# Rebuilding the prologue of a fused adaLN, attention and SwiGLU kernel: scale rows first, four head groups over half the keys, filler products

## The chip, the cores and the metric

The kernel runs on one core of a Trainium2 chip. The metric is the device time of one execution in microseconds (us). Three runs of the kernel before gave 1167.83, 1168.52 and 1172.24 us; the median, 1168.52 us, is the time before. The engines are named as the profile names them: PE (TensorE's matmuls), PEld (its weight loads), DVE (VectorE), ACT (ScalarE), POOL (GpSimd), SP (SyncE, which here issues nearly all DMAs).

## What is computed

```python
def reference(A_x, A_wq, A_wk, A_wv, A_wo, B_x, B_w1, B_w3, B_w2, c, w_mod):
    mod = (silu(c) @ w_mod).reshape(1, 6, 1, 1024)
    sa, ca, ga, sb, cb, gb = mod[:, 0], ..., mod[:, 5]      # shift, scale, gate; twice
    h = layernorm(x) * (1 + ca) + sa                        # x: 2048 tokens x 1024
    q = h @ wq   # 32 heads of 32      k = h @ wk, v = h @ wv   # one key and value head for all
    o = softmax(q k^T / sqrt(32)) v
    x = x + ga * (o @ wo)
    h = layernorm(x) * (1 + cb) + sb
    x = x + gb * ((silu(h @ w1) * (h @ w3)) @ w2)           # 1024 -> 3584 -> 1024
```

All tensors are bf16. The scale `1 + ca` and the shift `sa` are folded into the projections: the weights wq, wk and wv are multiplied by the scale, and the shift becomes a bias, `sa @ w`.

## The kernel before, in words

**A planner writes the order.** `build` adds every operation to a graph (`G.add`) with an engine, an estimated duration, a priority (`prio`, smaller is earlier) and the buffers it reads and writes. `Dag.schedule` (L106 to L260) plays the graph through with these estimates and fixes one order for each engine; `emit` writes the five instruction streams with semaphores. At run time each engine goes through its own list in order, and an instruction that has to wait holds up all that stand behind it. `LOOK` (L205) is a switch that lets the planner hold back a long DVE instruction; it is 0 in this version.

**Prologue (L452 to L762).** SP loads the 16 tiles of x (128 tokens each) into 8 slots of X and, between them, eight 128-row pieces of the first 2048 columns of w_mod, which hold the shift and the scale together (`ORDER`, L644). silu(c) is laid out by a small transpose (L495). DVE takes mean and variance (L509, L511; for tiles 3 and 6 ACT does it, L519 and L523), POOL the reciprocal root (L530, L532), DVE normalizes (L544), PE transposes (L558), and ACT or DVE copies the transposed tile to HT (L569, L572). The products with w_mod (L677) fill one bank; from it come `1 + ca` (L687) and the shift (L689). Then the bias products (L693, L699, L707, later L741), the scaling of wk, wv and wq (L719, L721, L750), the key projections (L608), the value projections (L619) and the query projections (L629). The gates and the second modulation follow (L782, L809, L787, L794).

**Attention (L830 to L959).** Eight blocks of 256 queries. For each block, eight head groups f of four heads. One *step* s takes 256 keys: eight score products (L855) into PSUM banks of SP, then two exponentials of 128x1024 on ACT (L865) into a ring U of 11 buffers. Eight steps make a head group. DVE adds the eight exponentials up in two trees (L879, L884) and folds these (L889); PE multiplies the exponentials by V (L902) and the tree sum by a 0/1 matrix SEL (L922), which gives the denominators. DVE copies both (L929, L937, L940), takes reciprocals (L946), spreads them (L952) and divides (L957). A block has 128 exponentials, the kernel 1024.

**Post (L982 to L1084).** For each block the product with wo (L996), the residual (L1000), the second layernorm, the gate and up products (L1030, 448 a block), tanh on ACT (L1039, 14 a block), the down products (L1064, 224 a block) and the output. Its weights stream through a ring of six buffers in WREG, HREG and X. The planner sets the post of block b among the attention steps of block b+1. Six PSUM banks belong to the scores once attention runs; everything else then shares banks 0 and 1.

Of the kernel before, what the change touches and what calls it, by code (L numbers as in the profile page):

```python
# [8 lines left out]
P = 128  # L9
# [3 lines left out]
LOOK = 0.0  # L13
# [15 lines left out]
class Dag:  # L29


    def __init__(self, nc):
        self.nc = nc
        self.nodes = []
        self.last_write = {}
        self.readers = {}
        self.seq = 0
        self.dma_sems = {}
        self.last_acq = {}
        self.chain = 0  # L40

# [64 lines left out]
    def schedule(self, banks):  # L106
# [41 lines left out]
        while left:  # L148
# [56 lines left out]
            if e == "dve" and LOOK and n.dur > 0.9 and n.prio > 1:  # L205
                fin = None
                for b in banks:
                    g = bank_group[b]
                    rem = [x for x in g.nodes if x.start is None and x.eng == "pe"] if g is not None else []
                    if rem:  # L210
                        f1 = t_free["pe"] + sum(x.dur for x in rem) + 0.26
                        if fin is None or f1 < fin:
                            fin = f1
                if fin is not None and t < fin < t + LOOK:
                    t_free["dve"] = fin
                    continue
            ready[e].remove(n)
# [132 lines left out]
def build(nc, x_in, wq_in, wk_in, wv_in, wo_in, w1_in, w3_in, w2_in, c_in, wmod_in, out, S, D, F):  # L350
# [34 lines left out]
    BP = (0, 0, 0)  # L385
    WP = (4, 4, 4)
    RP = (0, 0, 0)
# [6 lines left out]
    RB = sb("RB", [P, QB], F32)  # L394
    WKR = sb("WKR", [P, NC, 4, 32], BF16)
    ASB = XN[:, 2:4, :].rearrange("p a d -> p (a d)").bitcast(F32).rearrange("p (a q) -> p a q", a=4)
    DSB = WKR[:].rearrange("p c a f -> p (c a f)").bitcast(F32).rearrange("p (a q) -> p a q", a=2)
# [25 lines left out]
    NR = len(RING)  # L423
    assert NF * QB + 2 * 4096 <= NC * S and NXS == 8
# [5 lines left out]
    WQ0R = WKR[:].rearrange("p c a f -> p c (a f)")  # L430
    WQ0K = ["WKR"]
# [20 lines left out]

    cuts = {}
    G.add("pool", lambda e: e.memset(SEL[:], 0.0), writes=["SEL"], dur=0.3)
    for a, fs in enumerate(DGRP):
        edge = [32 * j // len(fs) for j in range(len(fs) + 1)]
        for j, f in enumerate(fs):
# [4 lines left out]
    G.add("pool", lambda e: e.memset(IDENT[:], 0.0), writes=["IDENT"], dur=0.2)  # L462
    G.add("pool", lambda e: e.affine_select(IDENT[:], IDENT[:], pattern=[[-1, P]], compare_op=ALU.not_equal,
                                            fill=1.0, base=0, channel_multiplier=1),
          reads=["IDENT"], writes=["IDENT"], dur=0.4)

# [5 lines left out]
    def xload(t0, n):  # L472
        r = []
        for t in range(t0, t0 + n):
            r.append(dma(lambda e, t=t: e.dma_start(X[:, t % NXS, :], x2[t * P:(t + 1) * P, :]),
                         ("x", t % NXS), writes=[("X", t % NXS)], nbytes=P * D * 2))
        return r

    WQK = [("WREG", "q")]
    xload(0, 8)  # L480

    def wmload(k, after=()):
        return dma(lambda e, k=k: e.dma_start(WM01[:, k, :], wmod_in[k * P:(k + 1) * P, 0:2 * D]), ("wm01", k),
            writes=[("UR", k)], nbytes=P * 2 * D * 2, after=after)
# [50 lines left out]
    def xnt(q):  # L535

        return XN[:, q, :] if q < 4 else UREG[:, (NU + NTR - 2) * 2048 + (q - 4) * D:][:, 0:D]

    def xnk(q):
        return [] if q < 4 else [("UR", NU + NTR - 2 + (q - 4) // 2)]  # L540

    def ln_norm(t, q, s=None, bp=0):
        s = t % NXS if s is None else s
        G.add("dve", lambda e: e.tensor_scalar(xnt(q), X[:, s, :], MV[:, t, 0:1], RS[:, t:t + 1],  # L544
                                               ALU.subtract, ALU.mult),
              reads=[("X", s), ("RS", t), ("MV", t)], writes=[("XN", q)] + xnk(q), dur=0.42, prio=2 - bp)

    def ln_transpose(nt, q0, dst, dkeys, fs, fm, engs, prio=5, cbs=None, allow=None, bp=0):
# [3 lines left out]
        for cb in range(NC // ncb) if cbs is None else cbs:  # L552
            g = grp(allow)
            for i in range(nt):
# [6 lines left out]
                G.add("pe", tr, reads=[("XN", q0 + i), "IDENT"] + xnk(q0 + i), dur=ncb * 0.065, lat=0.2,  # L561
# [41 lines left out]
    def kproj(t0, n, allow=None):  # L603
        sl = slice(t0, t0 + n)

        def kmm(e, b, c):
            for gg in range(4):
                r = e.matmul(b[32 * gg:32 * gg + 32, 0:n], WKV[:, 0, c, :], HT[:, c, sl], start=c == 0, stop=c == NC - 1,  # L608
                             tile_position=(0, 32 * gg), skip_group_check=True)
            return r  # L610
        g = mm_group(NC, kmm, lambda c: WKK + hk(c, t0, n), n_cols=n, allow=allow, mode="V")
        G.add("dve", lambda e, g=g: e.tensor_scalar(KT[:, sl], PB[g.bank][:, 0:n], BIA[:, 0:1], None, ALU.add),
              reads=[("BIA", 0)], writes=[("KT", t) for t in range(t0 // 256, (t0 + n) // 256)], groups=[(g, "r")],
              dur=dve_t(n), prio=-5)

    def vproj(tb):
        def vmm(e, b, i):
            tt, c = i // NC, i % NC
            return e.matmul(b[:, tt * 32:(tt + 1) * 32], HT[:, c, tb * 512 + tt * P:tb * 512 + (tt + 1) * P],  # L619
                            WKV[:, 1, c, :], start=c == 0, stop=c == NC - 1)  # L620
        g = mm_group(4 * NC, vmm, lambda i: WVK + hk(i % NC, tb * 512, 512), n_cols=64, per=NC)
# [5 lines left out]
    def qproj(t0, n, f, allow=None):  # L627
# [3 lines left out]
                     lambda c: [("WQ", min(f, 1), c)] + hk(c, t0, n) + WQK, n_cols=n, allow=allow)  # L631
        G.add("dve", lambda e, g=g: e.tensor_scalar(QT[:, f, sl], PB[g.bank][:, 0:n], BIA[:, f + 1:f + 2], None, ALU.add),
              reads=[("BIA", min(f + 1, 2))],
# [5 lines left out]
    ONACT = (3, 6)  # L639
    TR2A, TR2B = (0, 1, 2, 3), ()  # L640
    Q1ST = 1
    TR2E = ("act",)
    TR3E = ("act",)
    ORDER = ("w0", "w1", "w2", "w3", "x8", "x9", "w4", "x10", "x11", "w5", "w6", "w7", "q", "x12", "x13", "x14", "x15")  # L644

    def ln(t):
        (ln_stats_act if t in ONACT else ln_stats)(t)
        ln_scale(t, 1)
        ln_norm(t, t % 8)

    def tr(t0, nt, cbs, engs, allow=None):
        G.chain = 3
        ln_transpose(nt, t0 % 8, lambda c: HT[:, c, t0 * P:(t0 + nt) * P], lambda c: htk(c, t0 * P, nt * P), None, None,
                     engs, cbs=cbs, allow=allow)
        G.chain = 0
# [3 lines left out]
    for o in ORDER:  # L659
        if o[0] == "w":  # L660
            prev = [wmload(int(o[1:]), after=prev)]
        elif o == "q":
            prev = [dma(lambda e: e.dma_start(WQ0R, wq_in[:, 0:P].rearrange("(c p) f -> p c f", p=P)), "wq0",
                        writes=WQ0K, nbytes=P * D * 2, after=prev)]
        else:
            t = int(o[1:])
            while done_ln < t - 7:
                ln(done_ln)
                done_ln += 1
            prev = [dma(lambda e, t=t: e.dma_start(X[:, t % NXS, :], x2[t * P:(t + 1) * P, :]), ("x", t % NXS),  # L670
                        writes=[("X", t % NXS)], nbytes=P * D * 2, after=prev)]
    xl = prev
    g = grp((0,))
    for k in range(NC):
        def mm(e, k=k, g=g):
            for j in range(16):
                i = e.matmul(PB[g.bank][:, j:j + 1], WM01[:, k, j * P:(j + 1) * P], SCT[:, k:k + 1],  # L677
                             start=(k == 0 and j == 0), stop=True, skip_group_check=True)
            return i
        G.add("pe", mm, reads=["SCT", ("UR", k)], dur=16 * 0.06, lat=0.2, acq=g if k == 0 else None,  # L680
              groups=[(g, "w")], mode="F")
    tr(0, 4, None, ("act", "dve"), (2, 3, 4, 5))
    tr(4, 4, None, ("act", "dve"), (2, 3, 4, 5, 6, 7))
    for t in range(8, 12):
        ln(t)
    tr(8, 4, TR2A, TR2E, (6, 7))
    G.add("dve", lambda e, g=g: e.tensor_scalar(MODC[:, 1, :], PB[g.bank][:, 8:16], 1.0, None, ALU.add),  # L687
          writes=[("MODC", 1)], groups=[(g, "r")], dur=0.13, prio=-1)
    G.add("dve", lambda e, g=g: e.tensor_copy(SAB[:], PB[g.bank][:, 0:8]), writes=["SAB"],  # L689
          groups=[(g, "r")], dur=0.13, prio=-1)  # L690
    bia = grp((1,))
    for c in range(NC):
        G.add("pe", lambda e, c=c: e.matmul(PB[bia.bank][:, 1:2], WQ0R[:, c, :], SAB[:, c:c + 1], start=c == 0,  # L693
                                            stop=True, skip_group_check=True),
              reads=["SAB"] + WQ0K, dur=0.06, lat=0.2, acq=bia if c == 0 else None, groups=[(bia, "w")], mode="F")

    def vbmm(e):
        for c in range(NC):
            r = e.matmul(PB[bia.bank][:, 16:48], SAB[:, c:c + 1].broadcast_to([P, P]), WKV[:, 1, c, :], start=False,  # L699
                         stop=True, skip_group_check=True)  # L700
        return r
    G.add("pe", vbmm, reads=["SAB"] + WVK, dur=0.5, lat=0.2, groups=[(bia, "w")], mode="F")

    def kbmm(e):
        for c in range(NC):
            for gg in range(4):
                r = e.matmul(PB[bia.bank][32 * gg:32 * gg + 32, 0:1], WKV[:, 0, c, :], SAB[:, c:c + 1], start=False,  # L707
                             stop=True, tile_position=(0, 32 * gg), skip_group_check=True)
        return r
    G.add("pe", kbmm, reads=["SAB"] + WKK, dur=0.6, lat=0.2, groups=[(bia, "w")], mode="V")  # L710
    G.add("dve", lambda e: e.tensor_copy(BIA[:, 0:2], PB[bia.bank][:, 0:2]), writes=[("BIA", 0), ("BIA", 1)],
          groups=[(bia, "r")], dur=0.13, prio=0)
    G.add("dve", lambda e: e.tensor_copy(VB[:], PB[bia.bank][:, 16:48]), writes=["VB"],
          groups=[(bia, "r")], dur=0.13, prio=0)
# [430 lines left out]
```

## Time and profile before

| What | Value |
|---|---|
| three runs | 1167.83, 1168.52, 1172.24 us |
| the profiled execution: its own time | 1172.46 us |
| its span | 1170.7 us |
| mean granted PE clock | 0.981 |
| PE busy | 1124.0 us (96%), 15561 matmuls |
| ACT busy | 1028.9 us (88%) |
| DVE busy | 1013.7 us (87%) |
| first exponential starts | 36.41 us |
| last exponential ends | 1060.45 us |
| HBM read | 201.46 MB |

The rows of a timeline give start, duration, engine, line, operation, output<-inputs and a count; in brackets stands how long the engine had been idle and what ended the wait. A window row gives the busy time of each engine in a stretch, the granted clock and the DMA rate. A busy PE need not be a PE at its peak, since the ends of matmuls are modelled.

### The profile page before, as it was taken

Reading aid. Unit: us, or ns where it says so; the run is one execution under the profiler, and the core shown is the slowest. Engines: PE = TensorE matmul, PEld = TensorE weight load, DVE = VectorE, ACT = ScalarE, POOL = GpSimd, SP = SyncE. Lnnn points to the kernel's source line nnn. Section 1 sums busy time; section 2 is a strip of 40 time slices with the busy share of each in tenths; the row PEclk is TensorE's granted clock in tenths of the full one; section 3 lists DMA queues with packets and bytes.
Section 4 is the critical chain, followed back from the end, with each engine's and each line's share of the span. In section 5 each row is a group of like instructions: output and inputs, shape, how many; then the busy total and the mean of one; then the engine's idle time right before and its main releaser. Section 6 shows DMA issues by size and latency. Waiting matters only on the chain.

```text
span 1170.7 us, 34975 instructions
## 1 busy us (share of the span) xinstructions
PE 1124.0 (96%) x15561; PEld 757.9 (65%) x15561; DVE 1013.7 (87%) x1504; ACT 1028.9 (88%) x1174; POOL 43.1 (4%) x86
## 2 busy tenths in 40 slices
PE   4898997999989999999999999999999999999998
PEld 4554442667656676676666766767666757677887
DVE  7687988898988999899989998999989998997451
ACT  3798999899999999999999999999999999992110
POOL 5100000000010001000000001000100000000000
PEclk9897998899999999999999999999999999999999
DMA  9606007365757565966587566856596658656996
GB/s 348 216 23 196 19 2 181 109 181 160 200 129 211 169 169 133 278 182 170 156 233 204 164 179 175 246 166 174 144 257 176 191 145 246 198 161 176 299 291 154
DMA packets 383222, 211.05 MB, mean 180 GB/s; under 512 B 21600, under 2 KB 374880, under 8 KB 383072
## 3 DMA queue, kind: packets, MB, share of 16 engines
q1 hardware_dynamic: 380992, 208.69, 63.4%
q8 instruction: 122, 2.00, 0.7%
q10 hardware_dynamic: 2080, 0.13, 0.1%
q14 instruction: 28, 0.23, 0.1%
HBM read 201.46 MB, written 4.19 MB: 176 GB/s over the span
## 4 chain that ended last, share of the span: by engine, by line
PE 74%; ACT 15%; DVE 8%; issue 2%; POOL 1%; DMA 0%; SPq 0%
PE PB L1030 23%; PE PB L1064 15%; ACT UREG L865 14%; PE SP L855 11%; PE PB L902 9%; PE PB L629 4%; PE PB L996 4%; PE SP L1030 3%; DVE UREG L884 2%; PE SP L1064 2%; DVE UREG L879 1%; PE PB L922 1%; PE PB L608 1%; DVE HREG L1042 1%; PE SP L558 1%
## 5 line engine op out<-in xcount | busy, mean ns | idle before, releaser
L865 ACT ACTIVATE UREG<-SP 128x1024 bf16<-128x1024 f32 x1024 | 974.3, 1113 | 21.1 <-PE SP L855 18.8
L884 DVE TENSOR_TENSOR UREG<-UREG 128x2048 bf16<-128x2048 bf16 x256 | 311.9, 1218 | 11.6 <-ACT UREG L865 9.4
L855 PE MATMUL SP<-QT,KT 32*128 32x256 bf16 x4096 | 206.4, 276 | 16.4 <-ACT UREG L865 15.8
L1030 PE MATMUL PB<-QT,WREG 128*128 128x256 bf16 x1632 | 205.6, 273 | 0.8 <-DVE WKR L940 0.4
L1030 PEld LDWEIGHTS PB<-QT,WREG 128*128 128x128 bf16 x1632 | 148.2, 98 | 47.1 <-issue 31.7
L879 DVE TENSOR_TENSOR UREG<-UREG 128x2048 bf16<-128x2048 bf16 x128 | 156.2, 1220 | 13.2 <-ACT UREG L865 9.6
L855 PEld LDWEIGHTS SP<-QT,KT 32*128 32x128 bf16 x4096 | 61.0, 92 | 141.0 <-ACT UREG L865 91.8
L902 PE MATMUL PB<-UREG,V 128*32 128x256 bf16 x4032 | 134.1, 282 | 1.4 <-ACT UREG L865 1.4
L1030 PE MATMUL PB<-QT,HREG 128*128 128x256 bf16 x1056 | 132.9, 273 | 0.7 <-DVE WKR L940 0.4
L902 PEld LDWEIGHTS PB<-UREG,V 128*32 128x32 bf16 x4032 | 101.2, 99 | 28.4 <-issue 17.5
L1030 PEld LDWEIGHTS PB<-QT,HREG 128*128 128x128 bf16 x1056 | 96.1, 98 | 29.7 <-issue 19.7
L1064 PE MATMUL PB<-WREG,HREG 128*128 128x256 bf16 x840 | 104.9, 273 | 0.5 <-DVE HREG L1042 0.5
L1064 PEld LDWEIGHTS PB<-WREG,HREG 128*128 128x128 bf16 x840 | 77.8, 98 | 22.2 <-issue 12.6
L1030 PE MATMUL PB<-QT,X 128*128 128x256 bf16 x544 | 69.1, 273 | 1.1 <-DVE WREG L1037 0.7
L629 PE MATMUL PB<-HREG,WREG 128*128 128x512 bf16 (+1 forms) x312 | 67.8, 355 | 1.8 <-ACT HREG L569 0.9
L889 DVE TENSOR_TENSOR UREG<-UREG 128x2048 bf16<-128x2048 bf16 x56 | 68.2, 1218 | 0.4
L1064 PE MATMUL PB<-HREG 128*128 128x256 bf16 x532 | 67.1, 273 | 0.0
L1039 ACT ACTIVATE GSB<-GSB 128x512 bf16<-128x512 bf16 x56 | 41.6, 742 | 28.1 <-DVE GSB L1037 28.1
L929 DVE COPY XN<-PB 128x256 f32<-128x256 f32 x63 | 26.6, 422 | 39.8 <-PE PB L922 38.0
L1039 ACT ACTIVATE WREG<-WREG 128x512 bf16<-128x512 bf16 x56 | 42.8, 765 | 20.1 <-DVE WREG L1037 20.1
L1030 PEld LDWEIGHTS PB<-QT,X 128*128 128x128 bf16 x544 | 49.8, 98 | 15.9 <-issue 10.7
L996 PE MATMUL PB<-WO,QT 128*128 128x512 bf16 x232 | 57.8, 381 | 0.4 <-DVE WREG L1070 0.4
(130 smaller groups left out, 1004.2 us busy)
## 6 DMA issues: line engine op xcount, KB each, us to landing
WREG<-in_B_w_dram SPq DMA_DIRECT2D x112, 512.0 KB, 5.1
HREG<-in_B_w_dram SPq DMA_DIRECT2D x74, 512.0 KB, 5.4
WREG<-in_B_w_dram SPq DMA_DIRECT2D x33, 896.0 KB, 5.2
X<-in_B_w_dram SPq DMA_DIRECT2D x38, 512.0 KB, 5.0
HREG<-in_B_w_dram SPq DMA_DIRECT2D x21, 896.0 KB, 5.3
X<-in_B_w_dram SPq DMA_DIRECT2D x10, 896.0 KB, 5.0
X<-in_A_x_dram SPq DMA_DIRECT2D x32, 256.0 KB, 5.6
WREG<-in_w_mod_dram SPq DMA_DIRECT2D x16, 512.0 KB, 5.2
```

The costliest lines, as they stand in the source:

```text
L629: g = mm_group(NC, lambda e, b, c: e.matmul(b[:, 0:n], WQ[:, c, f * P:(f + 1) * P], HT[:, c, sl], start=c == 0, stop=c == NC - 1), lambda ...
L855: r = e.matmul(SP[:, b, o:o + qn], KT[32 * gg:32 * gg + 32, kts[j] * P:(kts[j] + 1) * P], QT[32 * gg:32 * gg + 32, f, q0:q0 + qn], start=T ...
L865: G.add("act", lambda e, u=u, h0=h0, n=n, b0=b0, nb=nb: e.activation(U[:, u, h0 * W:(h0 + n) * W].rearrange("p (b w) -> p b w", b=nb), SP[ ...
L879: G.add("dve", lambda e, tr=tr, u=u, fu=first_u: e.tensor_tensor(TR[:, tr, 0:4 * W], U[:, fu, 0:4 * W], U[:, u, 0:4 * W], ALU.add), reads= ...
L884: G.add("dve", lambda e, tr=tr, u=u: e.tensor_tensor(TR[:, tr, 0:4 * W], TR[:, tr, 0:4 * W], U[:, u, 0:4 * W], ALU.add), reads=[("TR", tr) ...
L889: G.add("dve", lambda e, ta=ta, tb=tb: e.tensor_tensor(TR[:, ta, 0:4 * W], TR[:, ta, 0:4 * W], TR[:, tb, 0:4 * W], ALU.add), reads=[("TR", ...
L902: r = e.matmul(PB[g.bank][32 * gg:32 * gg + 32, 0:qn], V[:, kt, :], U[:, pu, (gg * npk + j) * qn:(gg * npk + j + 1) * qn], start=w0 + n == ...
L929: G.add("dve", lambda e, g=g, f=f: e.tensor_copy(ASB[:, f % 4, 0:qn], PB[g.bank][:, 0:qn]), writes=[("ASB", f % 4), ("XN", 2 + f % 4 // 2) ...
L996: g = mm_group(NC, lambda e, b, f, t=t, h=h: e.matmul(b, QT[:, f, t * P:(t + 1) * P], WO[:, f, h * 512:(h + 1) * 512], start=f == 0, stop= ...
L1030: return e.matmul(b[:, j * qn:(j + 1) * qn], w13[:, w, c, j * P:(j + 1) * P], QT[:, c, q0:q0 + qn], start=c == 0, stop=c == NC - 1)
L1039: G.add("act", lambda e, b=b: e.activation(TB[b], GS[b], ACT.Tanh, scale=0.5), reads=[("GS", b)], writes=[("TB", b)], clear=alias("TB") if ...
L1064: G.add("pe", lambda e, g=g, j=j, fc=fc, hf=hf, first=first, w2s=w2s: e.matmul(PB[g.bank][:, j * 256:(j + 1) * 256], HHT[:, hf * NH + fc, ...
```

## The change

1. Modulation: each piece of w_mod is loaded as two halves of 1024 columns. All eight scale halves come ahead of all eight shift halves; wq is loaded in three cuts (128, 384 and 512 columns) into the WO buffer, from which scaled copies go to WQ. wk and wv get scaled copies too (WKS), so the bias products no longer need the unscaled weights to be kept in place.
2. All 16 casts of tiles 0 to 7 are on ACT, all 16 of tiles 8 to 15 on DVE (`EV`); before, ACT did 8 of the first 16 and all of the second. ACT takes the statistics of tiles 2 and 5, and scales four of the eight chunks of wq's second cut. Each of the 16 tiles has its own normalized buffer.
3. Block 0: head groups 0 to 3 attend to keys 0 to 1023 first, then to keys 1024 to 2047; groups 4 to 7 are as before. In these eight halves there are no DVE trees: SEL is multiplied by the exponentials themselves (`DIRECT`), 32 products a half.
4. Filler products: where the planner sees TensorE idle before its time 250, it puts products of the identity with itself into a free bank (`warm`).
5. The planner holds a DVE instruction of over 0.9 us back, if a finished bank or an urgent operation is due within 0.5 to 0.6 us (`LOOK`, `LK`, `LF`), in all blocks. The post of block 0 gets higher priorities (`BP`, `RP`), and its spreading of reciprocals gets four buffers (`RBQ`).

```diff
-LOOK = 0.0
+LOOK = 0.5
+LK = 0.6
+LF = 0.5
+UP = -1
...
-            if e == "dve" and LOOK and n.dur > 0.9 and n.prio > 1:
...
+            if e == "dve" and n.dur > 0.9 and n.prio > UP:
+                soon = [c for c in cands if c[1].prio <= UP and c[0] < t + LOOK]
+                if soon:
+                    t_free[e] = min(c[0] for c in soon)
+                    continue
...
+                if fin is not None and t < fin < t + LK:
+                    t_free[e] = fin
                     continue
+            if e == "pe" and self.warm is not None and t < self.warm[0]:
+                gap = s - t_free[e] - 0.3 - (0.1 if mode != "F" else 0.0) - (0.1 if n.mode != "F" else 0.0)
...
+                k = int(gap / self.warm[1])
...
-    BP = (0, 0, 0)
+    BP = (5, 0, 0)
-    RP = (0, 0, 0)
+    RP = (5, 0, 0)
...
+    WARM = 250.0
+    HEAD = 4
+    DIRECT = (0, 1)
...
-    ONACT = (3, 6)
+    ONACT = (2, 5)
+    QACT = 1
+    EV = (("act",), ("act",), ("dve",), ("dve",))
-    ORDER = ("w0", "w1", "w2", "w3", "x8", "x9", "w4", "x10", "x11", "w5", "w6", "w7", "q", "x12", "x13", "x14", "x15")
+    ORDER = ("x0", "x1", "x2", "x3", "x4", "x5", "a0", "a1", "x6", "a2", "a3", "x7", "a4", "a5", "a6", "a7", "q0",
+             "s0", "s1", "s2", "s3", "s4", "s5", "s6", "s7", "q1", "x8", "x9", "x10", "x11", "x12", "x13", "x14", "x15", "q2")
+    QCUT = (0, 1, HEAD, NC)
...
+    kproj(0, 256, (2, 3, 4, 5, 6, 7))
+    qproj(0, 256, 0, (2, 3, 4, 5, 6, 7), prio=1)
+    kproj(256, 256, (2, 3, 4, 5, 6, 7))
+    kproj(512, 512, (1,))
+    wscale(1, WVK)
+    qscale(1)
+    bias(1, (0,), vb=True)
+    qproj(0, 256, 1, (0, 1))
+    vproj(0, (0, 1))
+    vproj(1, (0, 1))
+    for f in range(2, HEAD):
+        qproj(0, 256, f, (0, 1))
+    tr(8, 4, (0, 1))
...
+        def step(f, s):
+            direct = q0 == 0 and f < HEAD and s // per_t in DIRECT
...
+            if direct:
+                return
...
+                            a = U[:, a[0]] if us else TR[:, a]
...
+        if q0 == 0:
+            head = []
+            for h in range(2):
+                for f in range(HEAD):
+                    head += [(f, s) for s in range(h * per_t, (h + 1) * per_t)] + [(f, (h,))]
+            sched = head + [x for x in sched if x[0] >= HEAD]
...
+    def warm(b, k):
+        def f(e):
+            for _ in range(k):
+                r = e.matmul(PB[b][:, 0:P], IDENT[:], IDENT[:], start=True, stop=True, skip_group_check=True)
+            return r
+        return f
+    G.warm = (WARM, P / 2400.0 + 0.0026, warm, ident)
```

The planner's order, which both versions fix before the run, shows what this moves. PE: 133 filler products, 110 of them ahead of the first score product and 23 in the post of block 0; SEL products 800 in place of 576. DVE: 120, 240 and 52 tree additions and folds in place of 128, 256 and 56; 16 casts in place of 8. ACT: 16 casts, then 4 scalings of wq, then 168 exponentials without a break before the first tanh; before, 16 casts, 10 exponentials, 4 casts, 1 exponential, 4 casts, and 161 exponentials. After the last score product the PE lists of both versions hold the same products: 224 down products of block 6, then the post of block 7.

## Prediction

> **What bounds the kernel now.** I read the 40 slices first, then a steady stretch of the windows, ACT's timeline for every break in the exponentials, and last the opening. Steady stretch:
>
> ```profile
> 400.00:600.00 200.00, 199.47 (x2840) 134.54 (x2829) 187.16 (x275) 198.82 (x224) 6.87 (x8) 1.00 0.66 180
> ```
>
> The columns are PE, PEld, DVE, ACT, POOL. ACT is full, 198.82 of 200, with 224 instructions. A block has 128 exponentials and 14 tanh, so 224/142 is 1.58 blocks and a block takes 126.8 us. PE shows 199.47, but "PEld SP L855 <- ACT UREG L865" is the longest wait on it, so ACT releases it. DVE has 6% left.
>
> ACT's timeline gives the pace (27.65/30 = 0.922 us an exponential) and the worst break:
>
> ```profile
> 36.41 9.52 ACT L865 ACTIVATE UREG<-SP 128x1024 bf16<-128x1024 f32 x10 [0.57 <-PE SP L855]
> ...
> 45.76 2.37 ACT L569 ACTIVATE HREG<-PB 128x512 bf16<-128x512 bf16 x4
> 48.01 1.03 ACT L865 ACTIVATE UREG<-SP 128x1024 bf16<-128x1024 f32 x1
> 48.92 2.09 ACT L569 ACTIVATE HREG<-PB 128x512 bf16<-128x512 bf16 x4
> 50.83 1.09 ACT L865 ACTIVATE UREG<-SP 128x1024 bf16<-128x1024 f32 x1
> 56.38 27.65 ACT L865 ACTIVATE UREG<-SP 128x1024 bf16<-128x1024 f32 x30 [4.46 <-PE SP L855]
> ```
>
> Read: 36 us without an exponential; ten; eight casts on the same engine; 4.46 us idle; the 13th exponential at 56.38. After it I add ACT's idle times in front of exponentials: 5.7 between 84 and 120, 5.0 between 175 and 215, 1.3 later, together 12.0. The last exponential ends at 1060.45; the rest, 110.25 us to 1170.7, is PE alone (down products of block 6, all of block 7's post).
>
> So the time is: start of the exponentials + 1024 of them and 98 tanh + breaks + tail. Only start and breaks can move. Tail and pace I cost at nothing: both versions' lists have the same products after the last score product.
>
> **Part 1: the first exponential.** Landing times: the windows give 220, 335, 397, 415, 414, 399, 399 GB/s for 2 us each from 2 us. The fourth piece of w_mod in before ends at 4.33 MB (wk and wv 0.13, eight x 2.10, four pieces 2.10), which is 13.9 us; its product starts after the DMA at 15.11, 1.2 later. In the changed order the last scale half ends at the same 4.33 MB: 15.1. The 128-column cut of wq (256-byte rows; at such a load the rate fell to 380 and 313 in before, about 0.2 MB worth) lands at 16.4, the last shift half (2.10 MB more at 0.40) at 21.5, the second cut of wq at 23.5. SP issues 26 loads by then at 0.46 us (eight x in 3.69), 12 us: hidden. Splitting w_mod adds eight issues at 0.46, hidden likewise. POOL's reordered constants take about 0.2 us each and end before its first use at 6.29.
>
> Two chains lead on. *PE and DVE:* PE stands before the last shift product; behind it in its list are key, bias and score products. Product 21.8, shift copy 22.15, bias products (0.40 and 0.38 in before) 22.95, two copies of 0.15, KT copy (0.48) 23.75, two wq scalings, QT copy 24.75, scores 25.2, exponential 25.6. *ACT:* 16 casts of 0.52 (2.06 for four) and four wq scalings (128x384, from the pace of the casts about 0.41, an estimate) stand before all exponentials. The second eight need tiles 6 and 7, and DVE normalizes these only behind the wq scaling that waits for 16.4: 1.22 + 0.42 + 2 x 0.5 give 19.2. Transposes, with shift products waiting between them: first bank 20.1. 8 x 0.52 + 4 x 0.41: 26.0. **First exponential 26.1, ACT's chain; 10.3 us earlier.**
>
> Does PE run at full rate there? The rows:
>
> ```profile
> 11.71 1.01 PE L558 MATMUL SP<-IDENT,XN 128*128 128x128 bf16 x8
> ...
> 34.10 0.61 PE L558 MATMUL SP<-IDENT,XN 128*128 128x128 bf16 x8
> ```
>
> The clock column says 1.00 up to 44 us, yet the same eight transposes took 1.01 at 11.71 and 0.61 at 34.10, a pitch of 0.108 against 0.056. The Trainium skill ("TensorE: Matmul & The Clock Gate", Part 1) says half rate is the default and about 3.4 us of sustained work lifts it. By the column the fillers buy nothing; by the rule 56 fillers in a row (6.0 us at 0.108) lift it by 10 us and the 42 that follow between scale products cost 42 x 0.056. The durations side with the rule, so I take full rate: scale products done 15.5, hidden. If the rate stays low, the fillers stand in front of the scale products: 98 x 0.108 + 22 transposes, done 19.8, and the first exponential is near 30. Bounds 26 and 30.
>
> **Part 2: to the 25th exponential.** Half the keys of four groups are 32 exponentials, so key tiles 8 to 15 are not needed at once. But the list puts the fourth group's query product (13th step) behind all 64 transposes of tiles 8 to 15, and those wait for DVE, in banks 0 and 1 only. DVE's list from 22.0 up to the last cast: 16 statistics x 0.61 = 9.8, 16 aggregates 1.0, 8 normalizations 4.0, 16 casts x 0.35 = 5.6, wq scalings 4 x 0.24 + 8 x 0.27 = 3.1 (896 columns took 0.374), bias copies 0.9, copies of KT, QT, V 3.6, one finished half 0.8: 28.8, with 0.6 of waits 51.4. Behind it on PE: two groups' V and SEL products (4 x 0.98), the query product 0.9, 12 key products 0.6; on DVE four copies and the QT copy; scores. 25th exponential at 57.05. ACT's first 24 end near 50.5: a break of 6.5 us takes the place of 4.46 and the casts. In before the 13th began at 56.38, so the gain here is 12 x 0.922 - 0.67 = **10.4 us**: the early start pays, the break stays.
>
> What may add to it is the clock:
>
> ```profile
> 44.00:46.00 2.00, 1.02 (x16) 0.37 (x14) 1.93 (x4) 2.00 (x4) 0.00 (x0) 0.56 0.64 198
> ...
> 48.00:50.00 2.00, 1.03 (x8) 0.77 (x8) 0.94 (x3) 2.00 (x5) 0.00 (x0) 0.50 0.21 52
> ...
> 52.00:54.00 2.00, 2.00 (x20) 0.66 (x22) 1.62 (x2) 0.00 (x0) 0.00 (x0) 0.50 0.00 0
> ```
>
> The third column from the right is the clock: it fell to 0.50 while PE did transposes at half occupancy, and came back only after 54. The same page (Part 4) says transposes do not count as activity for the gate. The changed kernel has twice as many transposes here, paced by DVE, and no fillers; the rule speaks against it. If the clock falls again, the 5.8 us of products up to step 13 take up to 3.5 longer; if step-wise scores and V products keep it up, nothing. I take 1.5 off.
>
> **Part 3: the other breaks.** Removed from DVE: 28 additions of groups 0 to 3, at 1.22 = 34 us, in a stretch (60 to 120) where it is 65 to 100% busy; added: eight copies of 0.42. Added to PE: 224 SEL products at 0.98/32 = 6.9 us. PE's remaining work up to the first tanh I add up to 132 us (72 steps x 0.33, query products 0.23 for 512 columns, 0.12 for 256, V and SEL 0.98 per 32), against 144 exponentials, 132.7 us: as full as ACT, so breaks do not all go. The 5.0 us at block 0's end come from here:
>
> ```profile
> 184.32 0.61 PE L855 MATMUL SP<-QT,KT 32*128 32x256 bf16 x8 [1.44 <-ACT UREG L865]
> ...
> 207.21 0.61 PE L558 MATMUL PB<-IDENT,XN 128*128 128x128 bf16 x4 [1.90 <-DVE XN L544]
> ```
>
> PE has nothing to do while DVE divides and normalizes, the clock falls (0.71 to 0.75 in these windows), scores take 0.61 for 0.40. In the changed list query products, 23 fillers and earlier divisions fill this; I expect 1 us. Of the 5.7 and 1.3 I expect 4.5. Breaks 12.0 to 5.5, bounds 1 and 12: **gain 6.5**. Loads of the first MLP weights now wait for query products five steps (9.2 us) ahead of their use; a weight load lands in 5.1 us: hidden, and a miss costs a few us once.
>
> **Sum.** 10.4 - 1.5 + 6.5 = 15.4 us. The profiled execution took 1172.46 (span 1170.7 and 1.76 around it): 1157.1. The median lies 3.94 lower: **1153.1 us**.
>
> **The rivals.** *A, the break grows:* the clock falls at 43 to 57 (3.5 us) and the fuller PE keeps 12 us of breaks: 10.4 - 3.5 = 6.9, 1161.6. For it: PE's 132 us against 132.7, and the rule on transposes. *B, the breaks vanish:* 1 us of breaks stays, and the 25th exponential comes 3 early because PE does V and SEL products while DVE casts: 10.4 + 11 + 3 = 24.4, 1144.1. Against it: both engines are full. *C, it does not do what it says:* fillers delay the scale (first exponential 30), and step 13 is bound by DVE anyway: about 1167. *D, slower:* the holding back of long DVE instructions costs in every block. DVE is busy 118.7 of 126.8 us a block, 8.1 free; 62 long instructions a block use that up at a mean hold of 0.13 us. At 0.20: 4.3 us a block over, times seven, 30: 1183. For it: it is the only part at work in all blocks. Against it: the list still has one addition between two copies, as before.
>
> **How the numbers follow.** Forecast 0.60 (own range 1146 to 1160), A 0.17, B 0.13, C 0.04, D 0.06. The range 1142 to 1163 takes in B and most of A. 0.5% is 5.8 us, about what a measurement of this kernel can tell from no change: faster than 1162.7 is the forecast, B and most of A, 0.86; same 0.08; slower 0.06.
>
> **What would show it.** First exponential at 26 (30: fillers in the way); a break near 50 to 57 before the 25th; transposes before 15 us at 0.6 for eight; clock in 43 to 57; ACT idle between 84 and 215 halved; a block of 126.8 us in 400 to 600 (more: rival D); 110 us after the last exponential. It is wrong if step 13 comes before 52 or after 62.

## The result and the profile after

| | before | after |
|---|---|---|
| median | 1170.38 us (4 runs, 1167.83 to 1172.74) | 1159.93 us (4 runs, 1159.58 to 1161.35) |
| profiled execution (span) | 1172.46 us (1170.7) | 1159.92 us (1158.1) |
| first exponential starts | 36.41 us | 29.21 us |
| last exponential ends | 1060.45 us | 1047.90 us |
| from there to the end | 110.2 us | 110.2 us |

The changed kernel is faster: the ratio is 0.9913, 95% interval 0.9886 to 0.9941. The forecast was 1153.1 (range 1142 to 1163); the time lies in the range, 6.8 us above it.

ACT's timeline of the changed kernel, up to the stretch that answers to 36.41 to 56.38 of before:

```profile
15.78 3.98 ACT L598 ACTIVATE HREG<-SP 128x512 bf16<-128x512 bf16 x8
22.52 4.20 ACT L598 ACTIVATE HREG<-SP 128x512 bf16<-128x512 bf16 x8 [2.75 <-PE SP L587]
26.60 2.12 ACT L741 ACTIVATE WREG<-WO,MODC 128x384 bf16<-128x384 bf16 x4
29.21 3.83 ACT L925 ACTIVATE UREG<-SP 128x1024 bf16<-128x1024 f32 x4 [0.49 <-PE SP L915]
35.60 7.44 ACT L925 ACTIVATE UREG<-SP 128x1024 bf16<-128x1024 f32 x8 [2.56 <-PE SP L915]
43.80 1.94 ACT L925 ACTIVATE UREG<-SP 128x1024 bf16<-128x1024 f32 x2 [0.76 <-PE SP L915]
47.02 9.27 ACT L925 ACTIVATE UREG<-SP 128x1024 bf16<-128x1024 f32 x10 [1.29 <-PE SP L915]
61.86 19.00 ACT L925 ACTIVATE UREG<-SP 128x1024 bf16<-128x1024 f32 x20 [5.57 <-PE SP L915]
```

The casts and scalings stand ahead of all exponentials, as planned; 24 exponentials have run before the long break, not 12, but there are four breaks where the forecast had one. PE's timeline has the clock that the forecast asked about, and the last shift product (L713, at 25.05):

```profile
14.56 0.61 PE L587 MATMUL SP<-IDENT,XN 128*128 128x128 bf16 x8
...
20.25 0.83 PE L637 MATMUL SP<-HREG,WKS 128*32 128x256 bf16 x12
...
22.11 1.01 PE L587 MATMUL SP<-IDENT,UREG 128*128 128x128 bf16 x8
...
25.05 0.40 PE L713 MATMUL PB<-SCT,UREG 128*128 128x1 bf16 x8
...
30.98 0.61 PE L637 MATMUL PB<-HREG,WKS 128*32 128x512 bf16 x6
32.98 1.26 PE L637 MATMUL PB<-HREG,WKS 128*32 128x512 bf16 x18 [1.39 <-issue]
...
43.68 1.90 PE L975 MATMUL PB<-UREG,V 128*32 128x256 bf16 x32
...
56.06 1.06 PE L975 MATMUL PB<-UREG,V 128*32 128x256 bf16 x32
```

Eight transposes at full rate before 15, at half rate at 22; V products at half rate at 43; and at 31.59 a wait of 1.39 us with no releaser. The windows show the same, and the rows of steady work and of block 0's end:

```profile
20.00:22.00 2.00, 2.00 (x40) 1.53 (x39) 0.38 (x1) 0.00 (x0) 0.00 (x0) 0.50 1.06 362
...
38.00:40.00 2.00, 1.01 (x36) 0.69 (x31) 2.00 (x5) 2.00 (x3) 0.00 (x0) 0.76 0.00 0
40.00:42.00 2.00, 1.66 (x42) 1.19 (x43) 2.00 (x10) 2.00 (x4) 1.23 (x5) 0.50 0.20 25
...
48.00:50.00 2.00, 1.46 (x28) 1.11 (x32) 2.00 (x8) 2.00 (x4) 0.81 (x2) 1.00 0.04 8
...
200.00:220.00 20.00, 20.00 (x278) 14.17 (x276) 19.77 (x25) 19.95 (x24) 0.00 (x0) 1.00 1.16 292
...
400.00:600.00 200.00, 199.19 (x2864) 134.64 (x2861) 185.06 (x273) 198.98 (x224) 6.86 (x8) 1.00 0.68 188
```

From 200 to 220, at block 0's end, the exponentials run without a break and the clock is 1.00 (before: 0.74), and a block takes what it took.

### The profile page after: what moved, and what is told of

It is laid out like the page before. It is cut to its first block, busy times and chain, and to the rows that moved or that the text cites. A ratio compares the mean times of both kernels' runs of the same rounds, so it can differ in the third digit from the quotient of the medians.

```text
span 1158.1 us, 35702 instructions
## 1 busy us (share of the span) xinstructions
PE 1122.6 (97%) x15918; PEld 767.1 (66%) x15918; DVE 984.7 (85%) x1498; ACT 1027.6 (89%) x1170; POOL 43.5 (4%) x86
## 4 chain that ended last, share of the span: by engine, by line
PE 92%; ACT 3%; DVE 3%; DMA 1%; SPq 1%; issue 0%; POOL 0%; DVEq 0%
PE PB L1141 33%; PE PB L1175 16%; PE SP L915 14%; PE PB L975 11%; PE PB L1107 5%; PE PB L658 4%; PE SP L1141 3%; ACT UREG L925 3%; PE SP L1175 2%; PE PB L1002 2%; DMA UREG<-in_w_mod_dram 1%; PE PB L637 1%; PE PB L838 0%; PE SP L1107 0%; DVE WO L850 0%
## 5 line engine op out<-in xcount | busy, mean ns | idle before, releaser
L925 ACT ACTIVATE UREG<-SP 128x1024 bf16<-128x1024 f32 x1024 | 968.6, 1075 | 18.8 <-PE SP L915 16.4
L948 DVE TENSOR_TENSOR UREG<-UREG 128x2048 bf16<-128x2048 bf16 x240 | 292.8, 1220 | 12.8 <-ACT UREG L925 10.8
L942 DVE TENSOR_TENSOR UREG<-UREG 128x2048 bf16<-128x2048 bf16 x120 | 146.4, 1220 | 11.5 <-PE PB L1002 6.4
L1175 PE MATMUL PB<-WREG,HREG 128*128 128x256 bf16 x812 | 101.2, 273 | 0.0
L1175 PEld LDWEIGHTS PB<-WREG,HREG 128*128 128x128 bf16 x812 | 75.3, 98 | 20.4 <-issue 11.4
L658 PE MATMUL PB<-HREG,WREG 128*128 128x512 bf16 (+1 forms) x312 | 64.1, 343 | 0.3 <-DVE DSB L1026 0.3
L957 DVE TENSOR_TENSOR UREG<-UREG 128x2048 bf16<-128x2048 bf16 x52 | 63.4, 1220 | 0.5
L1150 ACT ACTIVATE GSB<-GSB 128x512 bf16<-128x512 bf16 x56 | 38.8, 693 | 27.5 <-DVE GSB L1148 27.5
L1175 PEld LDWEIGHTS PB<-HREG 128*128 128x128 bf16 x532 | 49.2, 98 | 14.3 <-issue 8.0
```

Of the source, the lines that this page charges most:

```text
L658: g = mm_group(NC, lambda e, b, c: e.matmul(b[:, 0:n], WQ[:, c, f * P:(f + 1) * P], HT[:, c, sl], start=c == 0, stop=c == NC - 1), lambda ...
L925: G.add("act", lambda e, u=u, h0=h0, n=n, b0=b0, nb=nb: e.activation(U[:, u, h0 * W:(h0 + n) * W].rearrange("p (b w) -> p b w", b=nb), SP[ ...
L942: G.add("dve", lambda e, tr=tr, u=u, fu=first_u: e.tensor_tensor(TR[:, tr, 0:4 * W], U[:, fu, 0:4 * W], U[:, u, 0:4 * W], ALU.add), reads= ...
L948: G.add("dve", lambda e, tr=tr, u=u: e.tensor_tensor(TR[:, tr, 0:4 * W], TR[:, tr, 0:4 * W], U[:, u, 0:4 * W], ALU.add), reads=[("TR", tr) ...
L957: G.add("dve", lambda e, ta=ta, tb=tb: e.tensor_tensor(TR[:, ta, 0:4 * W], TR[:, ta, 0:4 * W], TR[:, tb, 0:4 * W], ALU.add), reads=[("TR", ...
L1150: G.add("act", lambda e, b=b: e.activation(TB[b], GS[b], ACT.Tanh, scale=0.5), reads=[("GS", b)], writes=[("TB", b)], clear=alias("TB") if ...
```

## The experiments

All are the changed kernel with one edit, unless said otherwise. Ratios are to the kernel before; the columns behind the median are of the one execution profiled. "25th" is the start of the 25th exponential, "end part" the time after the last exponential, "left over" the gate and up products that PE runs behind the last score product. (The expectations of e9 and e10 give 458, 605 and 491 for what the traces have as 450, 595 and 482.) In e3 to e8 and e10 to e12 the lists of PE, ACT and DVE are those of the changed kernel up to the first exponential, which starts at 28.50 to 29.91 there: differences below 1.4 us in that column say nothing.

| run | ratio, 95% interval | median us | first | 25th | last exp. ends | end part | left over |
|---|---|---|---|---|---|---|---|
| before | | 1170.38 | 36.41 | 67.25 | 1060.45 | 110.2 | 450 |
| after | 0.9913, 0.9886 to 0.9941 | 1159.93 | 29.21 | 61.86 | 1047.90 | 110.2 | 450 |
| e1 no fillers | 0.9930, 0.9908 to 0.9951 | 1161.83 | 27.99 | 60.91 | 1049.91 | 110.2 | 450 |
| e2 hold clock | 0.9932, 0.9914 to 0.9951 | 1161.56 | 32.05 | 63.76 | 1050.96 | 110.2 | 450 |
| e3 query first | 0.9960, 0.9944 to 0.9976 | 1164.46 | 29.91 | 58.23 | 1050.28 | 114.1 | 482 |
| e4 whole keys | 1.0143, 1.0120 to 1.0166 | 1186.29 | 28.68 | 74.30 | 1061.60 | 122.0 | 555 |
| e5 trees | 0.9956, 0.9940 to 0.9972 | 1164.22 | 29.39 | 65.41 | 1051.35 | 110.2 | 450 |
| e6 no hold | 1.0044, 1.0029 to 1.0058 | 1174.73 | 29.66 | 61.70 | 1047.39 | 126.6 | 595 |
| e7 no post | 0.9961, 0.9946 to 0.9975 | 1164.90 | 29.49 | 61.51 | 1047.09 | 115.0 | 482 |
| e8 hold 40 | 0.9922, 0.9905 to 0.9940 | 1160.43 | 29.33 | 60.62 | 1047.17 | 110.2 | 450 |
| e9 before + hold | 0.9997, 0.9985 to 1.0009 | 1169.86 | 36.12 | 66.75 | 1056.19 | 110.2 | 450 |
| e10 query, wp | 0.9922, 0.9903 to 0.9942 | 1160.63 | 28.50 | 56.00 | 1048.10 | 110.2 | 450 |
| e11 late x | 0.9900, 0.9881 to 0.9919 | 1158.55 | 29.46 | 52.89 | 1041.12 | 114.1 | 482 |
| e12 query, late | 0.9869, 0.9847 to 0.9891 | 1154.38 | 29.34 | 53.12 | 1043.92 | 110.2 | 450 |

**e1, the fillers left out.**

```diff
-            for _ in range(k):
+            for _ in range(0):
```

> The changed kernel with all 133 filler products taken out of TensorE's list and nothing else moved. Theory 1 (the fillers lift TensorE's rate only until about 18 us, and ACT's statistics and the loads decide the opening anyway): eight transposes near 14 us take 1.0 us in place of 0.61, the first exponential stays within 1.5 us of 29.2, the time within 2 us of 1159.9. Theory 2 (the fillers carry the opening): first exponential at 32 or later, time 1163 or more. In the post of block 0, without its 23 fillers, both leave up to 1 us.

Without fillers the transposes at 14.70 took 1.01, so fillers do lift the rate before 15 us. But the rate came without them by 18.7 and lasted to about 21.0, where the changed kernel lost it at 18.5; the first exponential came 1.2 us earlier, 0.5 below the lowest of the kernels with the same opening. Not all fillers are alike, though: without the 23 in the post of block 0 the clock is 0.83 from 185 to 205 us (1.00 with them), and ACT's breaks between 175 and 215 add up to 2.72 us in place of 0.93. In the total time the two kernels can't be told apart.

**e2, fillers behind seven modulation products.**

```diff
+    fill = lambda h, k: (6 if k > 4 else 0) if h else (12 if k < 4 else 0)
...
+                for _ in range(fill(h, k)):
+                    i = e.matmul(PB[g.bank][:, 256:384], IDENT[:], IDENT[:], start=False, stop=True, skip_group_check=True)
```

> The changed kernel with 66 more filler products: 6 behind each of the last three scale products, 12 behind each of the first four shift products, TensorE's order otherwise as it was. Theory 1 (the granted clock of 0.50 between 18.7 and 25 us is what makes the first exponential 3 us later than predicted): clock 1.00 there, eight transposes 0.61 in place of 1.01, first exponential at 26.5 to 27.5, time 1 to 2 us shorter than 1159.9. Theory 2 (DVE's normalizing of tiles 6 and 7 and the last shift load decide): first exponential at 28.5 to 29.5, time unchanged.

The clock stayed at 1.00 until 42, and eight shift products with eight transposes took 0.65 in place of 1.07. The first exponential came 2.8 us *later*: PE had two waits without a releaser, 0.68 and 1.55, which are 2.2 of it, and the fillers (0.83 for 12) stood in front of what they sped up. So the run doesn't tell what the half rate costs there: no run has that stretch at full rate without extra products in it.

**e8, fillers where PE does wait.** 8 and 18 filler products behind the first two value projections.

```diff
+            for _ in range((8, 18, 0, 0)[tb] if i == 4 * NC - 1 else 0):
+                r = e.matmul(b[:, 256:384], IDENT[:], IDENT[:], start=False, stop=True, skip_group_check=True)
```

> The order of every engine is that of the changed kernel; 8 and 18 filler products are put behind the products of the first two value projections (35.5 to 38.6 us), where PE then waits 0.64 and 1.33 us for ACT. Theory (the clock's fall at 39 to 45 costs: V products of 32 took 1.90 us there and 1.06 at 56, and DVE stood 1.62 us behind the SEL products): the clock stays at 1.00 between 38 and 46, the breaks of 0.76 and 1.29 go, DVE's casts start 1.5 earlier, and the 25th exponential comes 1.5 us earlier, at 60.3; 1158.3 us. Rival (PE's rate does not count there, as filling the slots at 18 to 24 did not bring the first exponential forward): the 25th exponential stays within 0.5 us of 61.9; 1160.

The windows of e8, to be read against 38 to 42 above:

```profile
38.00:40.00 2.00, 2.00 (x58) 1.74 (x54) 2.00 (x4) 1.48 (x2) 0.00 (x0) 1.00 0.04 8
40.00:42.00 2.00, 0.87 (x32) 0.54 (x25) 2.00 (x10) 1.82 (x2) 1.12 (x5) 1.00 0.17 46
42.00:44.00 2.00, 2.00 (x56) 1.52 (x56) 1.74 (x5) 2.00 (x4) 1.92 (x5) 1.00 0.53 146
```

The clock held, 32 V products took 1.06, and the 25th exponential came 1.24 us earlier (1.5 expected). A break of 1.51 at 116 (0.35 in the changed kernel) took most of that back; the last exponential ends 0.7 earlier, and the time did not move measurably. So a fall of the clock at 39 costs a little over 1 us locally.

**e3 and e10, the query products of groups 1 to 3 early**; e10 has `WP = (5, 4, 4)` besides.

```diff
-    qproj(0, 256, 1, (0, 1))
+    qproj(0, 256, 1, (0, 1), prio=1)
...
-        qproj(0, 256, f, (0, 1))
+        qproj(0, 256, f, (0, 1), prio=1)
```

> The changed kernel with the query products of head groups 1 to 3 at priority 1 in place of 5, so that the planner sets them ahead of the transposes of tiles 8 to 15. Theory 1 (the break of 5.6 us before the 25th exponential is one of order, but DVE's 29 us of work behind 22 us is what limits the second half of the keys): the 25th exponential near 55, but smaller breaks follow before the 33rd to 41st, and the time falls by 1 to 3 us. Theory 2 (order alone): 25th near 53 and no break behind it, time 5 to 6 us shorter, 1154 to 1155.

> The kernel with the query products of groups 1 to 3 early, and WP at 5 instead of 4 for block 0, which in the planner's list leaves 458 gate and up products behind the last score product where the early query products alone left 491. Theory (the early query products moved the 25th exponential forward by 3.6 us, and lost it to 33 products at the end, 3.7 us, and to a wait of PE for nothing visible, 2.7 us at 69): tail 110.2 instead of 114.1, so 1160.5; 1158 if the wait at 69 falls elsewhere. Rival (PE is as full as ACT, so what leaves the end comes back as breaks): 1164.

e3 brought the 25th forward by 3.6 us and was slower all the same. One reason is the end part: 32 more products left over, 3.9 us. e10 takes these back, and ends 3.8 us lower, as expected. The rest went to a wait of PE (2.67 us to 71.6 in e3, 2.33 to 69.0 in e10) and the break of over 4 us behind it.

**e4, whole keys and trees**, and **e5, halves with trees.**

```diff
-    DIRECT = (0, 1)
+    DIRECT = ()
...
-        if q0 == 0:        (e4 alone)
+        if False:
```

> The changed kernel with head groups 0 to 3 of block 0 attending to all keys in one go, as the other groups do, and so with their DVE trees again and without the SEL products on exponentials. Theory 1 (the half order is what feeds ACT while tiles 8 to 15 are prepared): after 8 exponentials ACT stands until the keys from 1024 are there, about 45 us; the 25th exponential comes near 68, the time is 6 to 8 us longer, 1166 to 1168. Theory 2 (the halves only move the break): 25th exponential within 2 us of 61.9, time within 2 us of 1159.9.

> Undoes one part: the halves keep their order, but the exponentials of head groups 0 to 3 are added up in DVE trees again (28 additions of 1.22 us, 34 us of DVE between 45 and 130) and SEL takes the sums (224 products fewer, 6.9 us of PE). The planner orders the rest anew. Theory (Part 3 of the prediction: DVE's additions made the breaks between 60 and 200): ACT's idle in front of exponentials between 70 and 200 grows from 2.8 us towards the 7.3 of before, so about 1164.5 us. Rival 1 (the halves alone removed these breaks, by leaving two key tiles' worth of work for later): within 2 us of the changed kernel, 1160. Rival 2 (the additions get in the way of the casts of tiles 8 to 15, as in the kernel with whole keys, where ACT stood 18.2 us): a break of over 10 us before the 25th exponential, 1168 or more.

e4 is slower than the kernel *before*. ACT stands 18.16 us in front of its 9th exponential (38.56 to 56.72), with DVE full (2.00 of 2 from 36 to 40 and from 44 to 50): whole keys need DVE's normalized tiles 8 to 15 at once, and the exponentials that come early only wait there. Both my numbers (1166 to 1168) were far off. Not all of the 26 us is the opening: the last exponential ends 13.7 us later, and 11.8 are the end part, with 105 more products left over. The longest break of e4, and that of e5:

```profile
56.72 3.77 ACT L925 ACTIVATE UREG<-SP 128x1024 bf16<-128x1024 f32 x4 [18.16 <-PE SP L915]
```

```profile
58.02 20.69 ACT L925 ACTIVATE UREG<-SP 128x1024 bf16<-128x1024 f32 x22 [10.32 <-PE SP L915]
```

e5 is 4.3 us slower than the changed kernel, the size that Part 3 gave, but not in its place: breaks after 70 grew by 1.1 us only (6.85 for 5.74), and a break of 10.32 ends at 58.02; the 25th exponential comes 3.6 us later. That is the mechanism of rival 2, at the theory's size.

**e6, no hold-back**, and **e9, the kernel before with the hold-back alone** (the planner's rule of the change and its constants, put into the kernel before). The edit of e6:

```diff
-LOOK = 0.5
-LK = 0.6
+LOOK = 0.0
+LK = 0.0
```

> Undoes one part: LOOK and LK at 0, long DVE instructions are never held back by the planner, in all blocks. Theory (the hold-back costs nothing and brings nothing, since a block takes 126.4 us with and without it): 1160, within 2 us of the changed kernel, and ACT's busy share in 400 to 600 stays at 199 of 200. Rival (the price of rival D, hidden by other gains): faster, 1155. Rival (the hold-back is what keeps the later blocks' breaks small): 1164 or more, with idle in front of exponentials after 200 above the 3.0 us that it is now.

> The kernel before, with one part of the change alone: its planner's rule for long DVE instructions and LOOK, LK, LF as in the changed kernel. Theory (in the changed kernel without that rule 605 gate and up products stood behind the last score product, with it 458, as in before; the rule is worth what its list leaves for the end, and before has nothing left over): 458 products there, tail 110 us, 1168.5, within 2 us of before. Rival (the rule removes waits of PE for DVE in every block, 7 blocks x 2 us): about 1156, and then the rule and not the prologue is what made the changed kernel faster.

Every theory of e6 missed: it is 14.8 us slower than the changed kernel, and slower than before. The third had "1164 or more", but not the place: breaks behind 200 us did grow, from 2.99 to 6.34, and yet the last exponential ends 0.5 us *earlier* than with the rule; all of the loss lies behind it. From 400 to 1000, e6:

```profile
400.00:1000.00 600.00, 588.15 (x8467) 400.08 (x8478) 553.84 (x806) 596.83 (x674) 14.88 (x20) 1.00 0.66 183
```

and the changed kernel:

```profile
400.00:1000.00 600.00, 597.97 (x8559) 407.67 (x8557) 555.90 (x808) 597.44 (x675) 17.16 (x20) 1.00 0.69 190
```

ACT is as full in both; PE is busy 9.8 us less in e6, since its list puts the post of each block later. 145 gate and up products more are left over, and the end part is 16.4 us longer: 0.113 us each, where their pitch is 0.109 (1.75 for 16). e3 (32, 3.9 us) and e4 (105, 11.8 us) fit the same line. In e9 the rule changes nothing (450 left over, as in before). It has no worth of its own; in the new order it decides what is left over.

**e7, the post of block 0 with its old priorities.**

```diff
-    BP = (5, 0, 0)
+    BP = (0, 0, 0)
...
-    RP = (5, 0, 0)
+    RP = (0, 0, 0)
```

> Undoes one part: the post of block 0 has its old priorities (BP and RP at 0). Theory (the break at block 0's end, about 5 us between 175 and 215 in the kernel before, went because the divisions and the second layernorm of block 0 now come earlier): the break comes back, 3 to 5 us between 175 and 215, 1164 us. Rival (query products and fillers that PE has there removed it): ACT's idle in 175 to 215 stays under 1 us, 1160.

The time is as the theory had it, the reason is not: ACT's breaks between 175 and 215 grew only from 0.93 to 2.27 us (5.0 in before), and the last exponential ends 0.8 *earlier* than in the changed kernel. The loss is the end part, 4.8 us longer, with 32 products left over (3.5 at that pitch).

**e11, late loads of x, and e12, e11 with e10's edits.** The last five loads wait for the first query copy:

```diff
+    loads(ORDER[:-5])
...
     qproj(0, 256, 0, (2, 3, 4, 5, 6, 7), prio=1)
+    loads(ORDER[-5:], [("QT", 0, 0)])
```

> The last four tiles of x and the last cut of wq are requested only once the first query copy is written (about 28 us instead of 20 to 23.4); the planner orders the rest anew, and leaves 491 gate and up products for the end. Theory (PE's waits without a releaser, 1.39 us at 31.6, are waits for its own program: they stand behind the 477th product in three kernels and behind the 348th and 478th in two with other counts, 128 apart, and end when the loads of x end at 31 to 33): with the DMA engines free from 27 to 30, the wait behind the 477th product is under 0.3 us, or gone. Rival (the wait has to do with the operation that stands there, or is none of the DMA's business): it stays at 1 us or more. The total: 1159 + 3.7 for the longer end, if the shorter break is gained; 1164 if the four late tiles hold up DVE.

> Early query products, WP at 5 for block 0 and the late loads together; 458 gate and up products behind the last score product. If all three theories hold: 25th exponential at about 57, no wait behind the 477th product, tail 110.2: 1156, faster than the changed kernel by 4. If PE's fullness takes it back as breaks between 70 and 400: 1160.

The waits without a releaser begin at fixed counts of products, whatever stands there. A window from the start to the wait counts them (first number in brackets). The changed kernel, then e2, then e10:

```profile
0.00:31.59 31.59, 24.81 (x477) 20.73 (x477) 19.35 (x50) 18.84 (x33) 11.47 (x39) 0.89 0.99 333
```

```profile
0.00:24.51 24.51, 19.05 (x350) 18.47 (x350) 14.29 (x33) 11.07 (x20) 11.29 (x38) 1.00 0.97 323
0.00:29.83 29.83, 23.69 (x478) 22.09 (x478) 16.44 (x43) 16.31 (x30) 11.29 (x38) 1.00 0.99 333
```

```profile
0.00:30.87 30.87, 24.24 (x477) 20.87 (x477) 19.24 (x50) 18.83 (x33) 12.54 (x39) 0.94 1.00 334
0.00:66.70 66.70, 54.75 (x1116) 40.06 (x1116) 45.12 (x117) 48.37 (x65) 18.76 (x54) 0.92 0.75 246
```

PE waits behind the 477th or 478th product in seven kernels (0.36 to 1.55 us), behind the 348th to 350th in e1, e2, e8 and e12 (0.68 to 0.84), behind the 1115th or 1116th in e2, e3, e5, e10, e11 and e12 (0.33 to 2.67): these places are 128 or nearly five times 128 apart, and a product is two instructions. The Trainium skill ("Runtime: NRT & Kernel Launch", Instruction fetch mechanics) says that an engine's program is fetched in blocks of 256 instructions, mostly hidden. The profile's instruction queue fits (packets, MB and share; the changed kernel, then before):

```profile
q8 instruction: 125, 2.05, 0.8%
```

```profile
q8 instruction: 122, 2.00, 0.7%
```

PE's 2 x 15918 instructions are 124.4 blocks of 256, those of before, 2 x 15561, are 121.6. And each of the 17 waits ends 2.3 to 2.7 us after a packet of this queue starts: in the changed kernel the packet starts at 30.29 and PE goes on at 32.98. e5 and e7 show no wait behind the 477th, but their packet starts at 29.30 and 0.3 to 0.4 us are hidden in the row of 24 products there (1.88 and 1.80 us, 1.48 in e11). In e11 the DMA engines have a share of 0.19 and 0.08 from 26 to 30. Its packet starts at 27.78, that of e12 at 27.68; in the nine kernels that pass this point with the loads of x running it starts at 28.96 to 30.75. PE goes through the point without a wait (e11, and e12 alike):

```profile
31.23 1.48 PE L637 MATMUL PB<-HREG,WKS 128*32 128x512 bf16 x24
```

and the break ahead of the fifth exponential is 0.78 in place of 2.56. So PE waits for its program, and the program comes late where loads of data fill the DMA engines. The time of e11 does not say what the late loads alone are worth, since its new order also puts the query products earlier: the 25th exponential comes 9 us earlier, and the last ends 6.8 us earlier, of which 3.9 go to 32 products left over. e12 leaves over no more than before and is the fastest, 1154.38 us; its interval (0.9847 to 0.9891) overlaps that of the changed kernel (0.9886 to 0.9941) by its edge only. Against e10, whose edits it has but for the late loads, it is 6.3 us faster, and the intervals are apart (e10: 0.9903 to 0.9942).

## Why the prediction was right, and where not

**The direction and the sum.** In the profiled execution 1157.1 was forecast and 1159.92 came, 2.8 us over. The other 4.0 of the 6.8 us are the last term, "the median lies 3.94 lower": the execution profiled of before lay near the top of its runs (1172.46; median 1170.38 later), that of after on its median. A profile's offset from a median of three is no constant to carry over.

**Part 1, first exponential 26.1: it came at 29.21.** The step that failed is the shift product at 21.8; the last one ran at 25.05. No shift product but the first waited for a DMA, so the loads of the shift halves are not it. Scale products ended near 17.2, not 15.5 (PE waited 0.95 us for a piece of w_mod), five of the eight shift products then stood behind 12 key products (20.25, 0.83 us), and from there shift products and transposes went at half rate: 1.07 us a pair of eight, 0.65 in e2, an estimated 1.7 us over four pairs. "I take full rate" held before 15 us and failed at 18.5. So the chain of PE and DVE, forecast at 25.6, ended last: ACT was through its own list at 28.72 (26.60 + 2.12) and stood 0.49 us for the score product. ACT's chain was late as well: its second eight casts began at 22.52, not 20.1, since the transposes stand in the same stretch of PE's list, and its scalings took 0.53 each, not 0.41. That 29.21 lies near the bound of 30 is chance: the bound was for scale products at half rate, and these ran at full rate.

**Part 2, gain 10.4 less 1.5.** The 25th exponential came 5.4 us earlier than in before (67.25), for a forecast 8.9. From the first to the 25th exponential the forecast gave 32.45 us (26.1 to 58.55 with the clock's 1.5), and 32.65 came: the miss of 3.3 us here (61.86 for 58.55) is Part 1's late start. The chain that the forecast named is the one that ran: DVE's last cast ended at 56.93, 31.45 us behind the shift copy (29.4 forecast), and the 25th exponential started 4.9 later (5.65). That the whole agrees to 0.2 us is partly chance, for the terms differ: the break ahead of the 25th was 5.57 for 6.5, three smaller breaks add 4.6, the clock was low from 39 to 46 and not at 43 to 57, and the program wait of 1.39 was not in the sum. The clock's price was right in size (1.24 by e8). The rule used for it, that transposes don't count, does not show here: 64 transposes from 48 to 56, and the clock at 1.00. In e1 the rate even rose by 18.7 behind a stretch from 13.83 that held only transposes and products with w_mod. Nor does PE's busy share in windows of 2 us tell the falls apart: it was 1.23 to 1.62 of 2 from 48 to 56, and 1.25 from 42 to 44 in before, ahead of its fall. What made the clock fall stays open.

**Part 3, gain 6.5.** The last exponential ends 12.55 us earlier, so behind the 25th 12.55 - 5.4 = 7.2 us were gained. (Breaks behind it are now 5.7 us, for 5.5; the 12.0 us that the forecast counted in before leave out ten of 0.25 us behind 450.) The reason given first was wrong: with the additions back on DVE (e5) the breaks from 70 to 200 stay small (3.2, before 7.3), and the additions cost ahead of that, among the casts. The order in halves is what counts: without it (e4) the rebuilt prologue is slower than the old one, and the exponentials end 10.3 us later than in e5, whose edit differs from e4's in that order alone. No run undoes the order of the loads or the move of the casts by itself; that these two bring the first exponential forward is read from the traces.

**The tail and the hold-back.** "Tail and pace I cost at nothing" holds for this list: 110.2 us and 198.98 of 200. But rival D had the wrong sign: the hold-back costs nothing in the blocks, and its *absence* costs 14.8 us, more than the whole gain, through what is left for the end. The lists before and after were counted, with the rule on; a count with the rule off would have shown 595.

**The fillers** bring nothing that can be measured in the time (e1): in the executions profiled the 110 of the opening cost about 1 us, and the 23 of block 0's end save 1.8 us of breaks. More of them can cost (e2).

## What to carry to other kernels

Where two engines are both full, an edit at the start is paid out at the end: count, in the order written, what the one engine has still to do when the other is done, with each switch of the change on and off, before a switch is costed at nothing. Work brought forward gains only up to the next thing that it needs: halving the keys made the early start usable, the early start alone lost. And where loads fill the DMA engines, a dense run of small products waits for its own program; move loads that are not yet needed out of its way before adding products to keep a clock up.

## What was not expected of the hardware

PE's waits for its program were 0.3 to 2.7 us, at the 128-product marks; just before them the DMA share was 0.95 (changed kernel, 30 to 32), 1.09 (e3, 66 to 69) and 1.08 (e11, 62 to 64). The granted clock reads 1.00 in the opening even where the rate is half: in e1 eight transposes took 1.01 at 14.70 with 1.00 in the column, as at 11.71 in before. And a fall was not ended by a busy PE at once: in the changed kernel PE was busy 2.00 of 2 from 20 to 24 at 0.50.
